# Attention and two expert layers on one core: row tiles 2 and 3 of the first batch spread over 16 half steps, and the next batch's bounds at other heads

## The chip, the core and the metric

The kernel runs on one core of a Trainium2 chip, as one program. Times are microseconds of device time. TensorE multiplies matrices into PSUM, VectorE and ScalarE work on SBUF and PSUM, GpSimd works on SBUF, and SyncE (SP) holds one queue that issues the DMAs of this kernel. Each engine runs its own instructions strictly in order and waits on semaphores for the others.

The number to predict is the median of several executions of the changed kernel. For the kernel before, three executions gave 873.21, 873.78 and 876.23, with the median 873.78.

## The reference

Causal attention with a decay per position comes first (4 batches, 8 heads, 576 positions, 64 wide), and its output, 2304 tokens of 512, goes through two layers with two weights each:

```python
def _attn_ref(q, k, v, f):
    scores = scale * np.matmul(q, k.transpose(0, 1, 3, 2))
    cum = np.cumsum(np.log(np.clip(f, 0.0001, 1.0)), axis=-1)
    scores = np.where(causal, -1000000000.0, scores + cum[:, :, :, None] - cum[:, :, None, :])
    attn = np.exp(scores - np.max(scores, axis=-1, keepdims=True))
    return np.matmul(attn / (np.sum(attn, axis=-1, keepdims=True) + 1e-09), v)

def _moe_ref(x, w_in, w_out):                 # 512 -> 2048 -> 512
    h = x @ w_in
    sp = np.where(h > 20.0, h, np.log1p(np.exp(np.minimum(h, 20.0))))
    return (h * np.tanh(sp)) @ w_out

def _moe2_ref(x, w_in, w_out, g_ln):          # 512 -> 1024 -> 512
    h = x @ w_in
    solu = h * softmax(h)
    return (layernorm(solu) * g_ln) @ w_out
```

The first layer is called MoE in the names. Its weights arrive as 64-bit floats.

## The kernel before

**Splits.** All products run in fp16 with every operand split into a high and a low half (`x = hi + lo`); three of the four products are kept. So each tile passes a cast (high half) and a subtract (low half), and each scale that keeps the halves in range is a power of two worked out from the data: for the weights from a bound per group, for q, k and v from squares summed over each batch (`stats`, `across`, `scales`).

**Attention.** The rows of a batch are cut into tiles 0 to 4 of up to 128 rows. `seq` lists *slots*: of tile 0 four heads make one slot, of tile 1 two, of tiles 2 to 4 one, so 2 + 4 + 8 + 8 + 8 = 30 slots for each batch. I write (3,7) for head 7 of row tile 3. A slot has the scores on TensorE (`step_s`, L409 to L412), the row max on VectorE and the exp on ScalarE (`step_r`, L451 and L453; for tile 4 L464 to L468), the high half by a cast (`step_h`, L491, in the first batch on ScalarE) and the low half on GpSimd (L492). Two heads share one tile `ph` and one transpose by DMA (L497, result `pT`). Three slots later (LAG = 3) come the products with v (`step_pv`, P.V, L523 to L525). After a row tile's last head `fin` scales the sum (x, L538), casts (L541) and subtracts (L542), and a DMA transposes the result into `xT` of the MoE block that holds these rows (L550). The next row tiles are prepared by `ahead`, head by head: raw q, k, v are loaded into a pool of three buffers, statistics are taken, scales are set, and the tiles are split.

**MoE blocks.** A block holds 256 tokens, so nine blocks in all; block 1 needs row tiles 2 and 3 of batch 0. A block has 16 units n. `up(n)` is 12 matmuls (L753), a pair of units shares the activation, called mish (`mish_a`, `mish_b`, `mish_c`: ScalarE L765 to L773, VectorE `ta` L770 and `th` L774, the cast to `gt` L779, its low half on GpSimd L780), and `down(n)` is six matmuls (L797). Block 0 runs while the weights are still prepared, in four groups of the two weights: load, conversion to fp32 by three bit operations on VectorE (L135, L137, L139), a Gram matmul (L158), the bound (L173 to L178), and the halves `win` and `wout` (L196 to L204), some on VectorE and ScalarE and some on ScalarE and GpSimd. The strings W1P and W2P set who does which half.

**The order of the work.** The code is one long loop over half steps. In each half step `hn` it issues an up or a down, up to four weight steps, and as many attention slots as `att_slots(hn)` asks for, a running total. That function spreads the cost of all slots evenly over EB = 190 half steps (`goal`), asks for enough slots in the last six half steps of a block that the next one can start (`lo`, from `need`), and never runs too far ahead (`hi`). The instructions are then put in order on each engine by a scheduler with a model of time, so that the order on the engines follows the code only roughly.

## Time and profile before

| | us |
|---|---|
| median of three executions | 873.78 |
| profiled execution | 870.92 |
| its span | 869.1 |
| TensorE busy in it | 747.8 (86%) |
| VectorE busy | 612.1 (70%) |
| ScalarE busy | 548.2 (63%) |
| GpSimd busy | 440.8 (51%) |

The span is the time from the first to the last instruction of the profiled execution. A busy share over the whole span is a mean over stages with different limits, so the stages are read apart: the first batch's preparation (to about 75 us), the weights of the MoE layer with block 0 beside them (to about 160), attention and blocks 1 to 8 (to about 550), the second layer's weights and the last blocks (to about 625), and the second layer.

### The profile page before, as it was taken

The numbers are of one execution on the slowest core, as the hardware profiler recorded it, in microseconds if no ns is written. First come the engines' busy times: TensorE is split into PE (matmuls) and PEld (weight loads), VectorE is DVE, ScalarE is ACT, GpSimd is POOL, SyncE is SP. The second block draws the span as 40 slices with busy tenths as digits, with TensorE's granted clock in tenths as the row PEclk, the third lists the DMA queues.
The fourth block names the chain that finished last, engine by engine and source line by source line (L and its number), as shares of the span: only waits on it lengthen the run. The fifth ranks groups of instructions, "written<-read, shape, count | busy, mean of one in ns | idle before, by whom it ended". The sixth has DMA issues, their size and how long they took to land.

```text
span 869.1 us, 16449 instructions
## 1 busy us (share of the span) xinstructions
PE 747.8 (86%) x6174; PEld 479.0 (55%) x6174; DVE 612.1 (70%) x1158; ACT 548.2 (63%) x1202; POOL 440.8 (51%) x341
## 2 busy tenths in 40 slices
PE   0546777778999989999888999986999999999997
PEld 0445445556667666677656766653555554444443
DVE  6799997577957978857896754689666454666451
ACT  5644638858778877698866767686965544333331
POOL 2269576635777678764777653227733132012110
PEclk9999887879999999999899999999999999999999
DMA  9999434668889799997897633761022523354543
GB/s 242 227 242 236 161 142 85 129 104 146 160 161 187 142 169 164 179 183 129 169 173 116 129 69 67 184 214 63 25 37 61 97 49 74 85 109 99 108 89 82
DMA packets 328571, 114.88 MB, mean 132 GB/s; under 512 B 317676, under 2 KB 317676, under 8 KB 328492
## 3 DMA queue, kind: packets, MB, share of 16 engines
q1 hardware_dynamic: 328492, 113.84, 62.5%
q8 instruction: 48, 0.79, 0.4%
q14 instruction: 31, 0.25, 0.1%
HBM read 46.59 MB, written 9.55 MB: 65 GB/s over the span
## 4 chain that ended last, share of the span: by engine, by line
PE 31%; DVE 25%; DMA 16%; ACT 9%; issue 9%; POOL 8%; SPq 1%; DVEq 0%; POOLq 0%; ACTq 0%
PE h L994 10%; PE o L1034 10%; DMA pT<-ph 6%; PE x L797 5%; PE h L753 4%; POOL ph L492 3%; DMA kt<-kn 2%; DVE ta L770 2%; DVE th L774 2%; DVE ph L489 2%; ACT p L453 2%; DMA w2i_r<-in_moe_w_in_dram 2%; DVE wout L137 1%; POOL gt L780 1%; DMA qa<-qn 1%
## 5 line engine op out<-in xcount | busy, mean ns | idle before, releaser
L753 PE MATMUL h<-xT,win 128*128 128x256 f16 x1728 | 225.0, 281 | 10.5 <-POOL win L204 4.0
L797 PE MATMUL x<-wout,gt 128*128 128x512 f16 x864 | 218.8, 387 | 16.2 <-ACT gt L779 5.9
L753 PEld LDWEIGHTS <-win 128*128 128x128 f16 x1728 | 170.9, 101 | 53.2 <-POOL win L204 4.2
L492 POOL TENSOR_TENSOR ph<-p,ph 128x512 f16<-128x512 f32 (+4 forms) x120 | 157.1, 1315 | 68.4 <-ACT ph L491 31.0
L780 POOL TENSOR_TENSOR gt<-th,gt 128x512 f16<-128x512 f32 x72 | 93.4, 1298 | 113.1 <-ACT gt L779 113.1
L797 PEld LDWEIGHTS <-gt 128*128 128x128 f16 x864 | 80.9, 100 | 94.7 <-issue 12.2
L1022 POOL TENSOR_TENSOR z<-sl,z 128x1024 f16<-128x1024 f32 x18 | 38.7, 2151 | 138.1 <-DVE s2c L1001 111.3
L523 PE MATMUL pv<-vt,pT 128*128 128x64 f16 (+3 forms) x480 | 72.7, 205 | 33.1 <-DMA pT<-ph 29.8
L994 PE MATMUL h<-w,x2T 128*128 128x512 f16 x432 | 98.4, 380 | 2.9 <-POOL w L204 1.6
L1034 PE MATMUL o<-wo,zT 128*128 128x512 f16 x432 | 96.5, 379 | 0.5 <-DMA zT<-z 0.5
L774 DVE SCALAR_TENSOR_TENSOR th<-ta,th 128x512 f32<-128x512 f32 x72 | 66.9, 930 | 27.6 <-ACT ta L773 27.3
L409 PE MATMUL sp<-kt,qa 128*128 128x128 f16 (+3 forms) x480 | 72.9, 225 | 13.4 <-ACT p L453 6.2
L453 ACT ACTIVATE p<-sp,nm 64x64 f32<-64x64 f32 (+7 forms) x128 | 61.2, 482 | 34.0 <-DVE nm L451 20.2
L523 PEld LDWEIGHTS <-pT 128*128 128x128 f16 (+3 forms) x480 | 46.5, 103 | 54.4 <-DMA pT<-ph 38.3
L410 PE MATMUL sp<-kt,qb 67*128 67x128 f16 (+3 forms) x480 | 73.7, 226 | 2.9 <-DVE qb L398 2.4
L770 DVE TENSOR_SCALAR ta<-ta 128x512 f32<-128x512 f32 x72 | 58.7, 815 | 21.8 <-ACT ta L765 21.5
L524 PE MATMUL pv<-vt,pT 128*128 128x64 f16 (+3 forms) x480 | 71.7, 200 | 0.6 <-DVE vt L197 0.6
L994 PEld LDWEIGHTS <-x2T 128*128 128x128 f16 x432 | 42.4, 98 | 53.9 <-issue 4.0
L525 PE MATMUL pv<-vt,pT 128*128 128x64 f16 (+3 forms) x480 | 71.8, 201 | 0.0
L1034 PEld LDWEIGHTS <-zT 128*128 128x128 f16 x432 | 42.2, 98 | 51.4 <-DMA zT<-z 0.9
L779 ACT CAST gt<-th 128x512 f16<-128x512 f32 x72 | 44.3, 615 | 41.3 <-DVE th L774 38.5
L771 ACT ACTIVATE ta<-ta 128x512 f32<-128x512 f32 x72 | 45.4, 631 | 35.0 <-DVE ta L770 34.8
(235 smaller groups left out, 1460.0 us busy)
## 6 DMA issues: line engine op xcount, KB each, us to landing
wi_r<-in_moe_w_in_dram SPq DMA_DIRECT2D x8, 1024.0 KB, 5.0
wo_r<-in_moe_w_out_dram SPq DMA_DIRECT2D x8, 1024.0 KB
rawk<-in_k_dram SPq DMA_DIRECT2D x25, 256.0 KB, 4.1
rawv<-in_v_dram SPq DMA_DIRECT2D x25, 256.0 KB, 4.1
x2d<-x2h SPq DMA_DIRECT2D x18, 256.0 KB, 2.4
out_dram<-ro SPq DMA_DIRECT2D x18, 256.0 KB, 2.0
w2i_r<-in_moe_w_in_dram SPq DMA_DIRECT2D x4, 1024.0 KB, 9.7
w2o_r<-in_moe_w_out_dram SPq DMA_DIRECT2D x4, 1024.0 KB, 5.0
```

The lines of the kernel that those rows point to most:

```text
L409: nc.tensor.matmul(o, qa[:, h, r0:r1_], kc[:, h, a0:a1], start=True, stop=False)
L410: nc.tensor.matmul(o, qb_[:67, h, r0:r1_], kc[:67, H + h, a0:a1], start=False, stop=(c != i))
L453: nc.scalar.activation(pv[:m, g * (i + 1) * P + off:g * (i + 1) * P + end], s3[:, g, off:end], AF.Exp, bias=nm[:m, g:g + 1], accum_out=rs[ ...
L492: nc.gpsimd.tensor_tensor(p4[:, :, 1], pv3, p4[:, :, 0], op=ALU.subtract)
L523: nc.tensor.matmul(o, pT[a0:a1, k, :m], vh, start=(c == 0), stop=False)
L753: nc.tensor.matmul(ph, win[:, (fi // 4) * NC1 + c, col:col + P], x[:, lx * NC1 + c, :], start=(m == 0), stop=(m == 3 * NC1 - 1))
L770: nc.vector.tensor_scalar(ta, ta, E20, 1.0, op0=ALU.min, op1=ALU.add)
L774: nc.vector.scalar_tensor_tensor(th, ta, 2.5, th, op0=ALU.subtract, op1=ALU.mult)
L780: nc.gpsimd.tensor_tensor(gt[:, 1], th, gt[:, 0], op=ALU.subtract)
L797: nc.tensor.matmul(o, gt[:, lg, n % 2, t * P:(t + 1) * P], wout[:, fi, lw * 512:(lw + 1) * 512], start=(first and m == 0), stop=(last and ...
L994: nc.tensor.matmul(h[:, half * 512:(half + 1) * 512], x[:, lx * NC1 + c, :], self.w2[:, half * NC1 + c, lw * 512:(lw + 1) * 512], start=(n ...
L1034: nc.tensor.matmul(o, zT[:, lz * NF2 + c, :], self.wo[:, c, lw * 512:(lw + 1) * 512], start=(n == 0), stop=(n == 3 * NF2 - 1))
```

## The change

Two things change. `att_slots` gets another lower limit in block 0: in each of its first 16 half steps (A0) one more slot is asked for, so that the 16 slots of row tiles 2 and 3 of batch 0 are issued at an even rate. Before, the even pace by cost set them. And `ahead` issues the loads, statistics and scales of the next batch's k and v at other heads: it counts from row tile 2 instead of tile 3, with the loads at counts 6, 8, 14, 15, 16, the statistics at 8, 10, 15, 16, 17, and the scales at 18. Counted in the same way, before they stood at 8, 10, 12, 14, 16, at 10, 12, 14, 16, 18, and at 19. The load of the next batch's row tile 0 goes from head 4 to head 3 of row tile 4, and its split from head 5 to head 4. The strings that set who does which half of the weights are the same in both.

```diff
+A0 = 16
...
-        if b + 1 < B and i in (3, 4):
-            n = (i - 3) * H + h
-            if n in (0, 2, 4, 6, 8):
-                load_raw(b + 1, n // 2, "kv")
-            if n in (2, 4, 6, 8, 10):
-                stats(b + 1, n // 2 - 1, "kv")
-            if n == 11:
+        if b + 1 < B and i in (2, 3, 4):
+            n = (i - 2) * H + h
+            if n in (6, 8, 14, 15, 16):
+                load_raw(b + 1, (6, 8, 14, 15, 16).index(n), "kv")
+            if n in (8, 10, 15, 16, 17):
+                stats(b + 1, (8, 10, 15, 16, 17).index(n), "kv")
+            if n == 18:
                 scales(b + 1, "kv")
         if nb < B:
-            if h == (LD if ni else 12 - H) and nb > 0:
+            if h == (LD if ni else 3) and nb > 0:
                 load_raw(nb, ni, "qkv")
...
-            if h == (LD + 2 if ni else 5):
+            if h == (LD + 2 if ni else 4):
...
         lo = need[j + 1] + LAG if j + 1 < NBLK and r >= 2 * NF1 - ATE else 0
+        if j == 0:
+            lo = max(lo, n0 + LAG + min(need[1] - n0, (r + 1) * (need[1] - n0) // A0))
         hi = need[j + XB] - 1 if j + XB < NBLK else len(seq) + LAG
```

The change adds one line at the top and two near the end, so a line L451 of before is L452 in the changed kernel, and L865 is L868.

The scheduler turns this into another order on the engines. Three places matter here. The first is VectorE around the bound of the last weight group of w_in, the row L178 before and L179 now (`wi_b`; `wo_r7` is the last raw tile of w_out, `nm_0_3_1` the row max of batch 0's head (3,1), `x32_0_2` the output of row tile 2). Before:

```order
L137 SCALAR_TENSOR_TENSOR wout_94<-wo_r7_881,wout_94 128x1024
L97 TENSOR_SCALAR wi_b_157<-wi_b_157 128x1
L770 TENSOR_SCALAR ta_4_1438<-ta_4_1438 128x512
L451 TENSOR_REDUCE nm_0_2_7_1026<-sp2_148 128x1
L451 TENSOR_REDUCE nm_0_3_0_1095<-sp0_146 128x1
L139 SCALAR_TENSOR_TENSOR wout_94<-wo_r7_881,wout_94 128x1024
L177 RECIPROCAL wi_b_157<-wi_b_157 128x1
L589 COPY wpt_83<-wi_b_157 128x1
L398 COPY qb0_126<-qa_0_4_1342 64x8x64
L197 SCALAR_TENSOR_TENSOR wout_94<-wout_94,wo_b_158 128x2x512
L535 TENSOR_SCALAR rr_0_2_1186<-rsum_0_2_613 128x8
L178 TENSOR_SCALAR wi_b_157<-wi_b_157 128x1
```

And now:

```order
L96 TENSOR_SCALAR wi_b_157<-wi_b_157 128x1
L198 SCALAR_TENSOR_TENSOR wout_94<-wout_94,wo_b_158 128x2x512
L452 TENSOR_REDUCE nm_0_3_0_1063<-sp0_146 128x1
L452 TENSOR_REDUCE nm_0_3_1_1090<-sp1_147 128x1
L542 CAST xh_0_2_1145<-x32_0_2_1143 128x512
L140 SCALAR_TENSOR_TENSOR wout_94<-wo_r7_917,wout_94 128x1024
L98 TENSOR_SCALAR wi_b_157<-wi_b_157 128x1
L775 SCALAR_TENSOR_TENSOR th_5_1660<-ta_5_1659,th_5_1660 128x512
L178 RECIPROCAL wi_b_157<-wi_b_157 128x1
L590 COPY wpt_83<-wi_b_157 128x1
L174 TENSOR_REDUCE wo_b_158<-gram_150 128x1
L179 TENSOR_SCALAR wi_b_157<-wi_b_157 128x1
```

The bound is the sixth row behind the last bit operation on the weights (L139, now L140) in both. Ahead of that operation the max of (3,1) and the cast of row tile 2's output have come in, and between it and the bound the `th` of units 10 and 11. Just above the second piece stand the `th` of units 8 and 9, the `ta` of units 10 and 11 and `x32_0_2`, all of which stood behind the bound before. The max of (2,7) moved further up.

The second place is GpSimd around the halves of the same group (`win_93` the halves of w_in, `wout_94` of w_out, `gt_4` the activation of units 8 and 9). Before:

```order
L201 TENSOR_SCALAR win_93<-win_93 128x2x512
L204 TENSOR_TENSOR win_93<-win_93 128x2x512
L542 TENSOR_TENSOR xh_0_2_1191<-x32_0_2_1189,xh_0_2_1191 128x512
L201 TENSOR_SCALAR wout_94<-wout_94 128x2x512
L201 TENSOR_SCALAR win_93<-win_93 128x2x512
L780 TENSOR_TENSOR gt_4_1482<-th_4_1439,gt_4_1482 128x512
L204 TENSOR_TENSOR wout_94<-wout_94 128x2x512
L492 TENSOR_TENSOR ph_0_3_0_1101<-p32_1_129,ph_0_3_0_1101 128x4x128
L492 TENSOR_TENSOR ph_0_3_2_1204<-p32_0_128,ph_0_3_2_1204 128x4x128
L204 TENSOR_TENSOR win_93<-win_93 128x2x512
L780 TENSOR_TENSOR gt_5_1676<-th_5_1593,gt_5_1676 128x512
```

And now:

```order
L781 TENSOR_TENSOR gt_4_1636<-th_4_1608,gt_4_1636 128x512
L543 TENSOR_TENSOR xh_0_2_1145<-x32_0_2_1143,xh_0_2_1145 128x512
L493 TENSOR_TENSOR ph_0_3_0_1066<-p32_0_128,ph_0_3_0_1066 128x4x128
L493 TENSOR_TENSOR ph_0_3_0_1066<-p32_1_129,ph_0_3_0_1066 128x4x128
L781 TENSOR_TENSOR gt_5_1689<-th_5_1660,gt_5_1689 128x512
L202 TENSOR_SCALAR win_93<-win_93 128x2x512
L205 TENSOR_TENSOR win_93<-win_93 128x2x512
L202 TENSOR_SCALAR wout_94<-wout_94 128x2x512
L202 TENSOR_SCALAR win_93<-win_93 128x2x512
L205 TENSOR_TENSOR wout_94<-wout_94 128x2x512
L493 TENSOR_TENSOR ph_0_3_2_1158<-p32_0_128,ph_0_3_2_1158 128x4x128
L205 TENSOR_TENSOR win_93<-win_93 128x2x512
```

Three splits are made here, of two rows each (L201 and L204). Before, row tile 2's output, a `gt` and two low halves of attention stood among them. Now two `gt`, row tile 2's output and two low halves of attention stand ahead of the first of them, and one low half among them.

The third place is ScalarE ahead of the exp of (3,7), the last head that block 1 needs (`ta_6` and `ta_7` are the mish of units 12 to 15, `jkv` the statistics of raw values). Before, behind the first mish step of `ta_6`, its partner L766 and the exp of (3,5):

```order
L313 ACTIVATE jkv_1_4_1641,st_1_1162<-rawv_1_4_1531 128x512
L771 ACTIVATE ta_6_1726<-ta_6_1726 128x512
L765 ACTIVATE ta_7_1863<-h_0_14_1751,usc1_0_79 128x512
L766 ACTIVATE th_7_1864<-h_0_14_1751 128x512
L453 ACTIVATE p32_0_128,rsum_0_3_1094<-sp0_146,nm_0_3_6_1435 128x512
L491 CAST ph_0_3_4_1312<-p32_1_129 128x4x128
L772 ACTIVATE ta_6_1726<-ta_6_1726,c_k1_72 128x512
L771 ACTIVATE ta_7_1863<-ta_7_1863 128x512
L491 CAST ph_0_3_6_1443<-p32_0_128 128x4x128
L773 ACTIVATE ta_6_1726<-ta_6_1726 128x512
L772 ACTIVATE ta_7_1863<-ta_7_1863,c_k1_72 128x512
L453 ACTIVATE p32_1_129,rsum_0_3_1094<-sp1_147,nm_0_3_7_1479 128x512
```

And now, from the first mish step of `ta_6` on:

```order
L766 ACTIVATE ta_6_1732<-h_0_12_1676,usc1_0_79 128x512
L767 ACTIVATE th_6_1733<-h_0_12_1676 128x512
L492 CAST ph_0_3_4_1238<-p32_1_129 128x4x128
L454 ACTIVATE p32_0_128,rsum_0_3_1062<-sp0_146,nm_0_3_6_1333 128x512
L772 ACTIVATE ta_6_1732<-ta_6_1732 128x512
L766 ACTIVATE ta_7_1863<-h_0_14_1757,usc1_0_79 128x512
L767 ACTIVATE th_7_1864<-h_0_14_1757 128x512
L492 CAST ph_0_3_6_1341<-p32_0_128 128x4x128
L773 ACTIVATE ta_6_1732<-ta_6_1732,c_k1_72 128x512
L454 ACTIVATE p32_1_129,rsum_0_3_1062<-sp1_147,nm_0_3_7_1374 128x512
```

The exp of (3,7) stood as the fourteenth instruction behind the first mish step of `ta_6`, and now stands as the ninth. The exp of (3,5), the statistics and three mish steps went to other places.

## Rows read from the trace of the kernel before

**Rows 1.** First line of the page: span and instructions of the profiled execution
```profile
span 869.1 us, 16449 instructions
```

**Rows 2.** Table of stretches: stretch, length, busy time by engine, clock, DMA share, GB/s
```profile
75.00:135.00 60.00, 43.91 (x332) 29.66 (x329) 59.02 (x76) 31.10 (x49) 40.42 (x20) 0.89 0.48 156
135.00:191.00 56.00, 40.02 (x408) 28.51 (x407) 34.71 (x83) 42.30 (x98) 34.93 (x26) 0.78 0.62 112
191.00:550.00 359.00, 331.70 (x3541) 237.38 (x3542) 269.00 (x490) 274.54 (x669) 235.62 (x209) 0.98 0.79 144
550.00:869.00 319.00, 303.13 (x1618) 158.46 (x1615) 186.96 (x401) 157.82 (x287) 94.98 (x56) 0.99 0.38 92
```

**Rows 3.** TensorE in time: start, us, line, output and inputs, count, [idle before]
```profile
155.27 1.49 PE L753 MATMUL h<-xT,win 128*128 128x256 f16 x12 [1.49 <-POOL win L204]
...
176.27 1.89 PE L797 MATMUL x<-wout,gt 128*128 128x512 f16 x8
...
178.00 0.19 PE L523 MATMUL pv<-vt,pT 128*128 128x64 f16 x1
...
191.42 0.82 PE L753 MATMUL h<-xT,win 128*128 128x256 f16 x3 [1.83 <-DMA xT<-xh]
```

**Rows 4.** GpSimd in time, same columns, 137 to 185 us
```profile
137.75 1.05 POOL L201 TENSOR_SCALAR win<-win 128x1024 f16<-128x1024 f32 x1 [0.41 <-ACT win L199]
...
143.10 1.16 POOL L542 TENSOR_TENSOR xh<-x,xh 128x512 f16<-128x512 f32 x1 [2.09 <-DVE xh L541]
...
146.25 1.59 POOL L780 TENSOR_TENSOR gt<-th,gt 128x512 f16<-128x512 f32 x1
...
149.88 2.27 POOL L492 TENSOR_TENSOR ph<-p,ph 128x512 f16<-128x512 f32 x2
...
152.11 3.10 POOL L204 TENSOR_TENSOR win<-win 128x1024 f16<-128x1024 f32 x1
...
168.84 2.51 POOL L492 TENSOR_TENSOR ph<-p,ph 128x512 f16<-128x512 f32 x2
...
184.68 1.72 POOL L542 TENSOR_TENSOR xh<-x,xh 128x512 f16<-128x512 f32 x1 [4.22 <-DVE xh L541]
```

**Rows 5.** VectorE in time, 116 to 181 us
```profile
116.14 0.54 DVE L451 TENSOR_REDUCE nm<-sp 128x1 f32<-128x384 f32 x1
...
116.61 2.61 DVE L139 SCALAR_TENSOR_TENSOR win<-wi_r,win 128x1024 int32<-128x1024 int32 x1
...
132.60 1.21 DVE L139 SCALAR_TENSOR_TENSOR wout<-wo_r,wout 128x1024 int32<-128x1024 int32 x1
...
136.06 0.14 DVE L178 TENSOR_SCALAR wi_b<-wi_b 128x1 f32<-128x1 f32 x1
...
140.22 1.33 DVE L774 SCALAR_TENSOR_TENSOR th<-ta,th 128x512 f32<-128x512 f32 x1
...
151.14 2.10 DVE L197 SCALAR_TENSOR_TENSOR wout<-wout,wo_b 128x1024 f16<-128x1024 f32 x1 [4.31 <-ACT wout L196]
...
157.73 1.11 DVE L770 TENSOR_SCALAR ta<-ta 128x512 f32<-128x512 f32 x1 [3.30 <-ACT ta L765]
...
158.89 0.69 DVE L451 TENSOR_REDUCE nm<-sp 128x1 f32<-128x512 f32 x1
...
180.40 0.68 DVE L538 TENSOR_TENSOR x<-pv,rr 128x512 f32<-128x512 f32 x1
```

**Rows 6.** ScalarE in time, 149 to 204 us
```profile
149.20 0.63 ACT L313 ACTIVATE jkv<-rawv 128x512 f32<-128x512 f32 x1 [1.72 <-DMA rawv<-in_v_dram]
...
157.01 0.69 ACT L765 ACTIVATE ta<-h,usc 128x512 f32<-128x512 f32 x1 [0.97 <-PE h L753]
...
164.88 0.70 ACT L453 ACTIVATE p<-sp,nm 128x512 f32<-128x512 f32 x1
...
203.24 0.31 ACT L453 ACTIVATE p<-sp,nm 64x64 f32<-64x64 f32 x1 [0.35 <-DVE nm L451]
```

**Rows 7.** Waits of TensorE: waiter, awaited, us in all, times, longest
```profile
PE pv L523 <- DMA pT<-ph: 29.8, 24, 3.5
```

## The prediction

> **What bounds the kernel now.** I read the table of stretches first, then the starts of TensorE's matmul groups, then the instructions of each engine between 100 and 205 us, and the order of both kernels at the same places. The span is 869.1 us [rows 1]. TensorE is busy 331.70 of the 359 us from 191 to 550, and 303.13 of the last 319 [rows 2]: there it is the bound, and an edit can win little. Before 191 it is not. Between 75 and 135 VectorE is, with 59.02 busy of 60: it converts the MoE weights, and attention and block 0 wait behind that. From 135 to 191 TensorE is busy only 40.02 of 56 us and VectorE 34.71: no engine is full, and what the reader is to see is a chain. The first ups that need the last weight group start at 155.27, after 1.49 of waiting for a half that GpSimd splits; block 1's first up starts at 191.42, after waiting for the transposed attention output xT [rows 3]. In the 36 us between, block 0 ends and slots of row tile 4 run. The chain that ends at 191.42, followed back: GpSimd's low half of the output at 184.68 [rows 4], the scaled output x on VectorE at 180.40 [rows 5], P.V of heads 6 and 7 of row tile 3 at 178.00 [rows 3], GpSimd's low half of head (3,7) at 168.84 [rows 4], its exp at 164.88 [rows 6], its row max at 158.89 [rows 5]. Row tile 3 is that late because head 6 of row tile 2 got its max only at 116.14, behind weight steps, and because several maxima of tile 3 stand behind a wout step at 151.14 that had waited 4.31 for ScalarE [rows 5]; ScalarE had stood still until 149.20 for a raw value load of the next batch [rows 6].
>
> The profiled execution took 870.92 us, its span and 1.8 around it; the median of the runs is 873.78, 2.86 higher. I sum against 870.92 and add 2.86 at the end. What starts block 1 earlier is handed on nearly whole: from the 24th up on TensorE's order is the same in both, and it is nearly full from there.
>
> **Row tiles 2 and 3 in 16 half steps.** The change issues one slot in each of block 0's first 16 half steps; no computation is added or removed. On VectorE the max of (2,6) moves ahead of a weight conversion, and (3,5) stands ahead of the wout step of 151.14 instead of behind it. The wout step itself I leave at 151: it still waits for ScalarE behind the statistics of a raw tile, whose load stands on SP behind a transpose of row tile 3. So the start of block 1 moves link by link:
> - The max of (3,7) follows the wout step (151.14 + 2.10) and (3,6), 0.69 each, so it is at about 154.6; before, it stood behind a ta that waited 3.30 for ups [rows 5]. From there ScalarE's order decides. Between its first mish step of units 12 and 13 at 157.01 and the exp of (3,7) at 164.88 [rows 6] lay 13 instructions, 7.87 / 13 = 0.61 each; now there are 8. The five that went (the exp of (3,5), a statistic, three mish steps) are 3.0. The mish step itself comes 0.7 earlier (154.5 against 155.2, under the last weight group below). I take 3.7 (1 to 4.4).
> - From that exp to the end of the low half were 5.2 us (168.84 and half of 2.51, [rows 4]). A gt of 1.1 that stood ahead on GpSimd now stands behind, and fewer exps of row tile 4 lie between on ScalarE. I take 1.5 (0 to 2).
> - From there to P.V were 7.9 us: the transpose, and downs in front of P.V on TensorE. The group now stands behind down 14, before behind down 16. Eight matmuls of downs took 1.89 at 176.27 [rows 3]; a down has six, so two are 2.8. The transpose may come later than these, so I take 1.9 (0 to 2.8).
> - From x at 180.40 to the low half at 184.68 [rows 4, 5] are 4.3 us. A row max (0.69) and a scaling of raw q, about as long, no longer stand between x and its cast: 1.4 (0 to 1.5).
> Sum: 3.7 + 1.5 + 1.9 + 1.4 = 8.5. Block 1 would start at about 182.9.
>
> The other half of the pace is batch 1's attention, whose first exp ran at 203.24 [rows 6]. It gains less: on ScalarE the scaling of the next q tile, which needs a load issued late, now stands before the exps of head (4,3), where it stood behind those of (4,5). I take 7 (0 to 9). TensorE alternates between both, so the end gains between 7 and 8.5; I take 7.7.
>
> **The last weight group.** Its bound on VectorE was ready at 136.06 [rows 5]. Ahead of it now stand two th steps (1.33 each), a ta (1.11), an x (0.68), its cast and one max (taken at 0.69 each); a max of heads (2,7), taken at 0.6, went away. 2 x 1.33 + 1.11 + 0.68 + 0.69 + 0.69 - 0.6 = 5.2 later. GpSimd took from 137.75 to 155.2 (152.11 + 3.10) over the halves of this group, with 2.09 idle and 1.16 + 1.59 + 2.27 = 5.0 of attention and gt work among them [rows 4]. All but one low half of that now stands ahead of them: 17.45 - 2.09 - 5.0 + 1.14 = 11.5 remain, and 137.75 + 5.2 + 11.5 = 154.5. I cost the edit at nothing beyond the 0.7 above; its cover is GpSimd's idle time and the rows that went ahead. Without that cover it costs the 5.2.
>
> **The bounds of the next batch.** As many loads, statistics and scales as before. Of the five pairs of loads the first three go earlier, the last two come in consecutive heads, and the scales come one head earlier, as do the load and the split of each next batch's first tile. On SP the early raw loads of batch 1 now stand ahead of weight loads and of the transpose of row tile 2's output; SP had room there. Two later boundaries follow (three with the first, which is in the sum above). TensorE's waits for attention transposes were 29.8 in 24, 1.24 each and 3.5 at the longest [rows 7]; one longest stop more or less at each boundary is -7.0 to +7.0, one mean stop -2.5 to +2.5. The rows are nearer to the mean, and loads bunch as much as scales gain: I take 0.
>
> **A rule weighed.** In the weight stretch an or of VectorE (two tiles in, one out) takes 2.61 at 116.61, when GpSimd works on a 128x1024 subtract, and 1.21 at 132.60, when it doesn't [rows 5]. Three attention subtracts, of heads (2,6), (2,7) and (3,0), move further into that stretch, where VectorE is full; I price one by 2.27 / 2 = 1.14 [rows 4].
> The Trainium skill, page "SBUF — State Buffer", section "Who interferes with whom", says that a VectorE instruction with two SBUF inputs and a GpSimd instruction that reads SBUF contend for one shared port pair, and that whoever comes first holds it for the whole instruction. By that rule each moved subtract is paid by VectorE in full, which the 2.61 against 1.21 bears out. It is the third rival.
>
> **Rivals.**
> - A slower one: the last weight group decides. If the gt steps and low halves that now stand ahead of it on GpSimd have to wait for ScalarE, the cover is gone: the last split ends 5.2 later, and all that follows it in order moves with it, up 12, the first mish step of its pair, and the exp of (3,7), which stands behind that on ScalarE. 873.78 + 5.2 = 879.0. For it: GpSimd's rows run in order, and 2.09 of its idle time there was a wait of this kind. Against: the 154.5 above. It decides once the last split ends after about 160.
> - No change: xT is earlier, but batch 1's attention is not, because ScalarE waits for raw q ahead of (4,3) and TensorE then stops at the first P.V of batch 1: 873.8 less 0 to 2.6. For it: the scaling of q moves ahead of three heads' exps. Against: the scales of batch 1, and with them its first q tile, come earlier as well.
> - VectorE pays for GpSimd: the bounds of groups 2 and 3 come three subtracts later, 3 x 1.14 = 3.4, and 7.7 - 3.4 = 4.3 of the gain remain: 869.5. For it: 2.61 against 1.21. Against: those subtracts met the same kind of step before, only later, so the sum of such meetings may not grow.
> - A bigger gain: the whole chain at its better ends (4.4 + 2 + 2.8 + 1.5 = 10.7) and a mean stop less at both boundaries, 2.5: 873.8 - 13.2 = 860.6.
>
> **How the numbers follow.** Forecast 870.92 - 7.7 + 2.86 = 866.1. Chances: forecast (a gain of 5 to 10) 0.43; half the gain by contention 0.14; a bigger gain 0.08; no change 0.16; slower 0.19. Two medians of this kernel can be told apart beyond 0.3%, 2.6 us. Faster: 0.43 + 0.14 + 0.08 = 0.65; same 0.16; slower 0.19. The range goes from a little beyond the bigger gain, since its two parts may meet the attention's gain of 9 as well, 858, to 877, most of the way to the slower rival; beyond these I leave 0.04 and 0.12. The likeliest case alone has 863 to 869.
>
> **What would show it.** Right: the max of (3,7) before 156 and its exp before 162, P.V of (3,6) by 171.5, block 1's first up between 181 and 185, batch 1's first exp by 198, and everything after 225 shifted by 6 to 9. For the weight step: the last split of win done by 156. Wrong: that split past 160 with block 0's last ups behind it (the slower rival); block 1 at 183, but a stop of over 4 us on TensorE before 225 (no change); ors and conversions of weight group 2 at 2.6 and more where they had 1.2 (contention). The forecast falls as a whole if TensorE's order after the 24th up isn't what carries the gain on: then block 1 starts early and a later stage stands where it stood.

## The result

The changed kernel took 861.34 us (858.52 to 864.30, four runs) against 874.56 before (873.21 to 876.23, four runs): a ratio of 0.9848, with an interval from 0.9809 to 0.9887. A second series gave 860.93 and 0.9856 (0.9824 to 0.9889). It is 13 us faster. Forecast were 7.7 less, 866.1, with 858 to 877 as the range, and 863 to 869 for the likeliest case: the range holds the time, the likeliest case does not. The profiled execution took 862.0, 8.9 less than the one of before, which at 870.92 had been quicker than most of its kind.

The head of the page of the changed kernel (span; then busy time, share and instructions of each engine), and its table of stretches, with the columns of [rows 2]:

```profile
span 860.2 us, 16457 instructions
...
PE 748.2 (87%) x6174; PEld 477.6 (56%) x6174; DVE 606.7 (71%) x1158; ACT 549.1 (64%) x1202; POOL 442.2 (51%) x341
```

```profile
75.00:135.00 60.00, 43.49 (x348) 30.28 (x346) 59.72 (x75) 33.79 (x54) 42.69 (x22) 0.91 0.59 176
135.00:191.00 56.00, 43.77 (x407) 30.03 (x405) 41.82 (x90) 42.30 (x97) 37.18 (x25) 0.79 0.61 115
191.00:550.00 359.00, 338.81 (x3588) 239.41 (x3588) 261.83 (x490) 276.72 (x670) 235.12 (x209) 0.98 0.79 148
550.00:860.00 310.00, 292.65 (x1568) 152.95 (x1565) 182.88 (x397) 152.98 (x277) 92.80 (x54) 0.99 0.37 87
```

TensorE's busy time is the same as before (748.2 against 747.8); what is gained is time in which it stood still, 9.3 us less than before in these two profiles. From 135 to 191 it is busy 43.77 against 40.02, from 191 to 550 338.81 against 331.70 [rows 2].

The links of the chain, engine by engine. TensorE, with the columns of [rows 3]: P.V of heads 6 and 7 of row tile 3, a stop, and block 1's first up.

```profile
172.53 0.19 PE L524 MATMUL pv<-vt,pT 128*128 128x64 f16 x1
...
181.71 0.22 PE L410 MATMUL sp<-kt,qa 128*64 128x128 f16 x1 [3.16 <-ACT p L469]
...
184.38 1.04 PE L754 MATMUL h<-xT,win 128*128 128x256 f16 x4
```

GpSimd, as [rows 4]: the last split of w_in, the low half of head (3,7), and the low half of row tile 3's output.

```profile
153.00 2.12 POOL L205 TENSOR_TENSOR win<-win 128x1024 f16<-128x1024 f32 x1
...
165.94 1.30 POOL L493 TENSOR_TENSOR ph<-p,ph 128x512 f16<-128x512 f32 x1 [1.90 <-ACT ph L492]
...
178.56 1.72 POOL L543 TENSOR_TENSOR xh<-x,xh 128x512 f16<-128x512 f32 x1 [1.80 <-DVE xh L542]
```

VectorE, as [rows 5]: the bound of the last group of w_in, the wout step, the max of (3,7), and the output of row tile 3.

```profile
141.59 0.14 DVE L179 TENSOR_SCALAR wi_b<-wi_b 128x1 f32<-128x1 f32 x1
...
153.14 3.06 DVE L198 SCALAR_TENSOR_TENSOR wout<-wout,wo_b 128x1024 f16<-128x1024 f32 x1 [1.86 <-ACT wout L197]
...
158.07 0.69 DVE L452 TENSOR_REDUCE nm<-sp 128x1 f32<-128x512 f32 x1 [1.26 <-ACT p L454]
...
175.30 0.69 DVE L539 TENSOR_TENSOR x<-pv,rr 128x512 f32<-128x512 f32 x1
```

ScalarE, as [rows 6]: the exp of (3,5), the first mish step of units 12 and 13, the exp of (3,7), the scalings of batch 1's second q tile and second k tile, and batch 1's first exp.

```profile
157.25 0.69 ACT L454 ACTIVATE p<-sp,nm 128x512 f32<-128x512 f32 x1 [2.75 <-POOL ph L493]
...
158.30 0.69 ACT L766 ACTIVATE ta<-h,usc 128x512 f32<-128x512 f32 x1 [0.26 <-PE h L754]
...
163.24 0.70 ACT L454 ACTIVATE p<-sp,nm 128x512 f32<-128x512 f32 x1
...
179.91 0.72 ACT L197 ACTIVATE qn<-rawq,scu 128x512 f16<-128x512 f32 x1 [3.33 <-DMA rawq<-in_q_dram]
...
183.28 0.71 ACT L197 ACTIVATE kn<-rawk,scu 128x512 f16<-128x512 f32 x1
...
199.40 0.31 ACT L454 ACTIVATE p<-sp,nm 64x64 f32<-64x64 f32 x1
```

| | before | predicted | after |
|---|---|---|---|
| bound of the last group of w_in | 136.06 | 141.3 | 141.59 |
| end of its last split | 155.2 | 154.5 | 155.12 |
| max of (3,7) | 158.89 | 154.6 | 158.07 |
| exp of (3,7) | 164.88 | 161.2 | 163.24 |
| end of its low half | 170.1 | 164.9 | 167.24 |
| P.V of (3,6) and (3,7) | 178.00 | 170.9 | 172.53 |
| output x of row tile 3 | 180.40 | 173.3 | 175.30 |
| its low half | 184.68 | 176.2 | 178.56 |
| block 1's first up | 191.42 | 182.9 | 184.38 |
| batch 1's first exp | 203.24 | 196.2 | 199.40 |

The chain is the one that was predicted, and its end within 1.5 us. Only its last link has changed: the first up no longer waits for xT, as no idle time stands before it at 184.38; it follows scores of row tile 4 that TensorE had reached after 3.16 of waiting for an exp. But the chain does not explain 13 us, and that it is handed on had to be tested.

### The profile page after: what moved, and what is told of

The parts are those of the page before. It is cut to its first block, busy times and chain, and to the rows that moved or that the text cites. A ratio compares the mean times of both kernels' runs of the same rounds, so it can differ in the third digit from the quotient of the medians.

```text
span 860.2 us, 16457 instructions
## 1 busy us (share of the span) xinstructions
PE 748.2 (87%) x6174; PEld 477.6 (56%) x6174; DVE 606.7 (71%) x1158; ACT 549.1 (64%) x1202; POOL 442.2 (51%) x341
## 4 chain that ended last, share of the span: by engine, by line
PE 40%; DVE 23%; DMA 13%; ACT 9%; issue 8%; POOL 7%; SPq 1%; POOLq 0%; DVEq 0%; ACTq 0%
PE h L997 10%; PE o L1037 10%; PE x L798 9%; PE h L754 7%; DMA pT<-ph 4%; POOL ph L493 4%; DVE th L775 3%; DVE ta L771 2%; DMA w2i_r<-in_moe_w_in_dram 1%; DVE wout L140 1%; PE pv L524 1%; DVE ph L490 1%; DVE wout L138 1%; POOL gt L781 1%; DMA rawk<-in_k_dram 1%
## 5 line engine op out<-in xcount | busy, mean ns | idle before, releaser
L798 PE MATMUL x<-wout,gt 128*128 128x512 f16 x864 | 222.1, 392 | 21.8 <-ACT gt L780 10.1
L493 POOL TENSOR_TENSOR ph<-p,ph 128x512 f16<-128x512 f32 (+4 forms) x120 | 159.6, 1334 | 80.3 <-ACT ph L492 32.8
L524 PE MATMUL pv<-vt,pT 128*128 128x64 f16 (+3 forms) x480 | 71.0, 203 | 15.4 <-DMA pT<-ph 10.7
L775 DVE SCALAR_TENSOR_TENSOR th<-ta,th 128x512 f32<-128x512 f32 x72 | 69.4, 965 | 21.1 <-ACT ta L774 20.9
L525 PE MATMUL pv<-vt,pT 128*128 128x64 f16 (+3 forms) x480 | 70.1, 198 | 1.0 <-DVE vt L198 1.0
L526 PE MATMUL pv<-vt,pT 128*128 128x64 f16 (+3 forms) x480 | 70.3, 198 | 0.0
L771 DVE TENSOR_SCALAR ta<-ta 128x512 f32<-128x512 f32 x72 | 53.7, 745 | 16.6 <-ACT ta L766 16.2
```

The source lines that it names most:

```text
L493: nc.gpsimd.tensor_tensor(p4[:, :, 1], pv3, p4[:, :, 0], op=ALU.subtract)
L524: nc.tensor.matmul(o, pT[a0:a1, k, :m], vh, start=(c == 0), stop=False)
L526: nc.tensor.matmul(o, pT[a0:a1, k + 1, :m], vh, start=False, stop=(c == i))
L771: nc.vector.tensor_scalar(ta, ta, E20, 1.0, op0=ALU.min, op1=ALU.add)
L775: nc.vector.scalar_tensor_tensor(th, ta, 2.5, th, op0=ALU.subtract, op1=ALU.mult)
L798: nc.tensor.matmul(o, gt[:, lg, n % 2, t * P:(t + 1) * P], wout[:, fi, lw * 512:(lw + 1) * 512], start=(first and m == 0), stop=(last and ...
```

## How the traces are compared

TensorE does the same matmuls in all kernels here, so its progress can be compared. As the reference serves a second profile of the kernel before, of 873.52 us, near the median (run e10 below). I sum the columns of all matmuls that the reference has started by a time, and ask how much earlier the other kernel had started the same sum. That is its *lead* at this time, in us; it counts attention and MoE alike. Each run is named by its parts: P the pace of block 0, F the new heads for the bounds of batch 1, L those for batches 2 and 3. The move of the load and the split of row tile 0 (from heads 4 and 5 to 3 and 4) is in all variants but the pace alone, and has no letter: without it the order is the same on every engine, instruction for instruction. Last come two columns of the rows themselves: the start of block 1's first up, and the first exp of batch 1's row tile 4.

```
lead in us at ...          210   230   260   340   400   430   530    up     exp
before, first profile      0.4   1.5   3.4   2.8   3.6   3.8   2.8   191.4  277.9
before, e10                  0     0     0     0     0     0     0   192.3  281.4
PFL (the change)           9.9   6.1   7.6   3.6   4.5  10.3  11.6   184.4  272.8
PFL, e1                   10.6   8.8   9.0   4.4   5.1  10.8  12.7   183.7  271.9
P, e2                     14.0   8.9   7.6   2.7   4.2   3.6   3.6   180.9  275.0
P, e11                    14.2   9.1   7.8   3.0   5.1   4.6   6.6   181.3  274.8
L, e3                      0.6  -0.3   3.1  -2.4  -3.2   1.9   3.5   192.6  277.9
PF, e4                     9.7   8.9   9.0   7.5   9.8   8.4  10.3   185.1  271.5
PF + batch 3 of L, e8     11.7   9.6  12.1   9.7  11.4  14.0  13.0   183.6  269.9
PL, e6                    15.1   9.1   8.2   3.6   2.8   5.5   2.9   180.3  275.1
FL, e7                    12.8   3.0   2.5  -3.0  -1.9   0.7   0.5   182.9  279.2
FL, e12                   12.1   2.3   1.6  -3.8  -2.7  -1.1   0.2   184.0  280.0
PFL, start delayed, e9     1.4   3.0   6.3   0.2   0.0   5.6   6.6   194.4  276.3
PFL, x delayed, e5         1.2   1.5   3.4  -4.2  -5.5  -1.9  -0.8   195.9  278.4
```

## The experiments

Theory A is the prediction's own: what block 1 gains at its start is handed on to the end. Its first rival, B, came from the first profile of the change, whose gain over the first profile of before shrank to about 1 us between 340 and 410 and came back at the boundary of batch 2 to batch 3.

**e1: the change again.** No edit.

> The changed kernel once more, for a second profile of it. Both theories expect 859 to 864 (0.982 to 0.988 of before). They differ in the trace. Theory A (handed on): what block 1 gains at its start, 7 us, is carried to the end; the fading of the lead to about 1 us between 340 and 410 us, which the first profile shows, is chance of that one execution, and in this profile TensorE's lead over the kernel before stays at 5 us or more from 230 to 410. Theory B (the last boundary): the lead fades here too, to 3 us or less between 340 and 410, and comes back to 8 or more after the boundary of batch 2 to batch 3 at about 415.

Measured: 860.93, 0.9856 (0.9824 to 0.9889). The lead falls to 4.4 at 340 (1.6 over the first profile of before) and comes back to 10.8 at 430 here too. So the fading is not chance; this claim of theory A fell.

**e2: the pace alone.**

```diff
# against the changed kernel: ahead() as in the kernel before
-        if b + 1 < B and i in (2, 3, 4):
+        if b + 1 < B and i in (3, 4):
...
```

> Only the 16 even half steps of block 0; loads, statistics and scales of the next batch at the heads of before, at all three boundaries. Theory A (handed on): block 1 starts 6 to 8 us earlier than before and the end gains 6 to 9: 0.990 to 0.993 of before, 865 to 868. Theory B (the last boundary): block 1 starts just as early, the lead fades before 410, and since the bounds are the old ones nothing comes back: 0.997 to 1.000, 871 to 875.

Measured: 867.91, 0.9929 (0.9906 to 0.9952), 6 us faster than before, as A had it and not as B had it. Block 1 starts 3 us earlier still than in the change.

**e3: the later bounds alone.**

```diff
# against the kernel before: the new heads only for batches 2 and 3
+        if b > 0 and b + 1 < B and i in (2, 3, 4):
...
-        if b + 1 < B and i in (3, 4):
+        if b == 0 and b + 1 < B and i in (3, 4):
```

> Block 0's pace and the bounds of batch 1 as in the kernel before; only the bounds of batches 2 and 3 at the new heads. On every engine the order is that of before up to about 240 us. Theory A (handed on): the start of block 1 is as before, so nothing is gained: 0.997 to 1.003, 871 to 877. Theory B (the last boundary): the stop of before at 412 to 417 (0.79 and 2.29) goes, and the end gains 4 to 8: 0.991 to 0.996, 866 to 870.

Measured: 873.71, 1.0011 (0.9985 to 1.0037). No gain, as A had it; B falls. The trace shows why B had seemed right: against e10 the new heads cost 6 us of lead between 260 and 400 and give it back by 530.

**e4: the pace with the bounds of batch 1.**

```diff
# against the changed kernel
-        if b + 1 < B and i in (2, 3, 4):
+        if b == 0 and b + 1 < B and i in (2, 3, 4):
...
+        if b > 0 and b + 1 < B and i in (3, 4):   # the heads of before
```

> The changed kernel with the bounds of batches 2 and 3 put back to the heads of before; the order is that of the changed kernel up to about 230 us on every engine. Theory A (handed on): the end keeps the start's gain: 860 to 866, within 3 us of the changed kernel. Theory B (the last boundary): the lead fades by 410 and does not come back: 868 to 873, 6 us or more above the changed kernel.

Measured: 864.93, 0.9894 (0.9863 to 0.9924). A's range holds, though not its "within 3 us" (it is 4 above the change); B's does not. The lead stays between 7.5 and 10.3 from 210 to the end. From here to the change are 4 us, from the pace alone 3; the intervals of neighbours overlap, so neither step is clear by itself.

**e5: the output of row tile 3 delayed on GpSimd.** The edit repeats one subtract, with the same result.

```diff
         nc.gpsimd.tensor_tensor(xh[:m, 1], x32[:m], xh[:m, 0], op=ALU.subtract)
+        for _ in range(4 if (b, i) == (0, 3) else 0):
+            nc.gpsimd.tensor_tensor(xh[:m, 1], x32[:m], xh[:m, 0], op=ALU.subtract)
```

> The changed kernel, in which GpSimd makes the low half of row tile 3's output five times instead of once: four times 1.15 to 1.7 more, 4.6 to 6.8 us, in the middle of the chain to block 1's first up, with nothing else added. Theory A (handed on): the first up starts 5 to 7 us later, at about 190, and the end is 3 to 7 us above the changed kernel: 864 to 868. Theory C (slack): the start of block 1 has slack, batch 1's attention sets the pace there, and the end is within 2 us of the changed kernel: 859 to 863.

Measured: 877.0, 1.0029 (1.0002 to 1.0056): 16 us above the change, more than either theory allows. GpSimd's rows (start, us), and SP's transpose of the output, show that the edit did more than it should (L545 are the extra subtracts, L493 low halves of row tile 4):

```profile
178.00 1.15 POOL L543 TENSOR_TENSOR xh<-x,xh 128x512 f16<-128x512 f32 x1 [1.81 <-DVE xh L542]
...
182.93 1.74 POOL L493 TENSOR_TENSOR ph<-p,ph 64x640 f16<-64x640 f32 x1 [0.97 <-ACT ph L492]
...
185.75 1.83 POOL L493 TENSOR_TENSOR ph<-p,ph 64x640 f16<-64x640 f32 x1
...
187.55 1.59 POOL L545 TENSOR_TENSOR xh<-x,xh 128x512 f16<-128x512 f32 x1
...
191.43 1.28 SPq L553 DMA_TRANSPOSE xT<-xh  x1
```

The extra subtracts stand among low halves of row tile 4, so attention waits as well; the transpose comes at 191.43, where e1 had it at 179.59. The run hits both streams and tells nothing of the start alone. e9 tries it in another way.

**e6: the pace with the later bounds only.**

```diff
# against the changed kernel: the new heads only for batches 2 and 3
-        if b + 1 < B and i in (2, 3, 4):
+        if b > 0 and b + 1 < B and i in (2, 3, 4):
...
```

> The changed kernel with only batch 1's bounds put back to the heads of before; batches 2 and 3 keep the new ones. Theory A (handed on), in the form the first four runs left it: without the early bounds the first q tile of batch 1 is scaled at about 182 instead of 173, TensorE waits for k and q of batch 1 near 199 and 217 as in the run with the pace alone, and the result is like that run: 0.991 to 0.995, 866 to 870. Theory D (three independent parts): the pace is worth 6, batch 1's bounds 3 and the later bounds 4, each alone, so this kernel gains 10: 0.987 to 0.990, 863 to 865.

Measured: 871.37, 0.9986 (0.9962 to 1.0010): no gain that can be told from none. Theory D falls; A named the mechanism (below), but it expected 4 us at least. On the pace alone the later bounds even cost 3.5 us (867.91 in e2, 871.37 here), and the two intervals do not overlap. Block 1's first up is the earliest of all runs, 180.3. Ten us lie between this kernel and the change, and all that differs is the bounds of batch 1.

What these do is seen in the second profile of the pace alone (e11). In the order of ScalarE the scalings of batch 1's first two q tiles and of its second k tile come late, and TensorE waits (start, us, line):

```profile
182.14 0.72 ACT L197 ACTIVATE qn<-rawq,scu 64x512 f16<-64x512 f32 x1
...
192.99 0.72 ACT L197 ACTIVATE qn<-rawq,scu 128x512 f16<-128x512 f32 x1
...
195.79 0.72 ACT L197 ACTIVATE kn<-rawk,scu 128x512 f16<-128x512 f32 x1
...
201.53 0.32 PE L410 MATMUL sp<-kt,qa 128*128 128x128 f16 x2 [2.74 <-DMA kt<-kn]
...
218.76 0.22 PE L411 MATMUL sp<-kt,qb 67*128 67x128 f16 x1 [1.69 <-DVE kt L375]
```

TensorE then stands 2.74 for k of row tile 1 and 1.69 for row tile 2. With the bounds early the two q tiles are scaled at 173.77 and 179.91 in the change, 8 and 13 us sooner, that k tile at 183.28 instead of 195.79, and these two stops are gone. In e6 they are there as in e11, with one more of 2.05 for k at 202.86 (TensorE):

```profile
200.33 0.32 PE L410 MATMUL sp<-kt,qa 128*128 128x128 f16 x2 [2.49 <-DMA kt<-kn]
...
218.81 0.22 PE L411 MATMUL sp<-kt,qb 67*128 67x128 f16 x1 [1.69 <-DVE kt L375]
```

**e7: all new bounds without the pace.**

```diff
# against the changed kernel
-        if j == 0:
-            lo = max(lo, n0 + LAG + min(need[1] - n0, (r + 1) * (need[1] - n0) // A0))
```

> All bounds at the new heads, without the even pace of block 0. Theory A (handed on): row tile 3 of batch 0 is as late as before, block 1 cannot start earlier, and early bounds of batch 1 meet attention that is not there yet: 0.997 to 1.003, 871 to 877. Theory D (three independent parts): 3 for the first bounds and 0 to 4 for the later ones, 0.992 to 0.997, 867 to 871.

Measured: 874.49, 1.0013 (0.9993 to 1.0034). The time is A's, the reason is not. A had expected block 1 to start late; it starts at 182.87, earlier than in the change, TensorE is 12.8 ahead at 210, and nothing of that reaches the end. In the rows of TensorE, SP's queue and ScalarE (the second q tile of batch 1, and the exp of (4,5)):

```profile
182.87 0.50 PE L754 MATMUL h<-xT,win 128*128 128x256 f16 x3
...
176.37 1.23 SPq L551 DMA_TRANSPOSE xT<-xh  x1
179.84 1.20 SPq L374 DMA_TRANSPOSE kt<-kn  x1
181.07 1.27 SPq L396 DMA_TRANSPOSE qa<-qn  x1
182.39 0.58 SPq L300 DMA_DIRECT2D rawq<-in_q_dram  x1
...
185.87 0.72 ACT L197 ACTIVATE qn<-rawq,scu 128x512 f16<-128x512 f32 x1 [0.53 <-DMA rawq<-in_q_dram]
...
188.28 0.29 ACT L468 ACTIVATE p<-sp,nm 64x64 f32<-64x64 f32 x1
```

SP issues the output's transpose first and the load of the second q tile at 182.39; ScalarE scales it at 185.87, and the exp of (4,5), behind it in order, is at 188.28, not earlier than in the kernel before (187.47 and 188.17 in its two profiles). In the change the same load is issued ahead of the output's transpose, at 175.83 in e1 (SP):

```profile
174.59 1.19 SPq L396 DMA_TRANSPOSE qa<-qn  x1
175.83 0.57 SPq L300 DMA_DIRECT2D rawq<-in_q_dram  x1
```

So here the early start and an attention as late as before come together, and the time is that of the rival called no change. That the one makes the other worthless is argued, not shown: TensorE's stops in this profile are 1.72 at 199.41 and 1.03 at 207.66 for transposes of row tile 4, and 1.74 at 222.67 for batch 1's row tile 1, none of them the single stop of over 4 us that the rival had named.

**e8: pace, and the bounds of batches 1 and 3.**

```diff
# against the changed kernel: batch 2 at the heads of before
-        if b + 1 < B and i in (2, 3, 4):
+        if b != 1 and b + 1 < B and i in (2, 3, 4):
...
+        if b == 1 and b + 1 < B and i in (3, 4):   # the heads of before
```

> The pace, and the bounds of batches 1 and 3 at the new heads, those of batch 2 at the heads of before. Up to about 370 us the order is that of the run without the later bounds, whose lead stayed near 6 there, while the changed kernel's faded to about 1 between 280 and 410. Theory E (a price at one boundary, a gain at the next): batch 2's new bounds cost 3 to 5 us between 280 and 340 and batch 3's give 3 to 5 after 410, so this kernel beats the changed one: 856 to 859. Theory A (handed on, the rest is chance of the order): it lands between the two, 861 to 866.

Measured: 861.81 (861.78 to 862.90), 0.9871 (0.9844 to 0.9898). That is in A's range and no better than the change, so batch 2's new heads neither cost nor give at the end and theory E's gain is not there, though the lead does what E said up to 400 (11.4 against 4.5 and 5.1). What the change has lost by then it makes up by 430; the stops that the kernel before has at that place (TensorE in e10) are absent from it.

```profile
417.40 0.19 PE L409 MATMUL sp<-kt,qa 128*64 128x64 f16 x1 [1.01 <-ACT p L468]
...
420.32 0.23 PE L523 MATMUL pv<-vt,pT 64*128 64x64 f16 x1 [2.31 <-DMA pT<-ph]
```

**e9: the start of block 1 delayed by a detour of its input.**

```diff
         nc.gpsimd.tensor_tensor(xh[:m, 1], x32[:m], xh[:m, 0], op=ALU.subtract)
+        if (b, i) == (0, 3):
+            for z in range(1):
+                nc.scalar.dma_start(dz, xh)      # dz: a new tile in DRAM
+                nc.scalar.dma_start(xh, dz)
```

> The changed kernel, in which the output of row tile 3 goes to DRAM and back before its transpose (two DMAs of 256 KB on ScalarE's queue): block 1's first up comes 4 to 6 us later, at 188 to 191, near where the kernel before had it, and batch 1's attention, with its bounds early, waits for nothing new; in TensorE's order its first scores now stand ahead of that up. Theory A (handed on): the start's 7 us are most of the gain, so the end is 4 to 6 us above the changed kernel: 865 to 868. Theory F (attention paces): the start of block 1 has slack as long as row tiles 1 to 3 of batch 1 come as early as in the changed kernel (first exp of row tile 3 at 243 to 246), and the end is within 2 us of it: 859 to 863.

Measured: 866.86, 0.9930 (0.9911 to 0.9950), 6 us above the change. The start came later than meant, 10 us behind the change and 2 to 3 behind the kernel before:

```profile
191.54 0.26 PE L525 MATMUL pv<-vt,pT 128*64 128x64 f16 x1 [3.96 <-DMA pT<-ph]
...
194.42 1.89 PE L759 MATMUL h<-xT,win 128*128 128x256 f16 x8
```

Yet the kernel is 6 us faster than before. A's time holds, though for a delay of 10 and not 4 to 6; F's does not, and its condition was not met either: batch 1's row tile 3 began at 246.95. Nor was attention left alone, as was meant: on ScalarE the second q tile of batch 1 is scaled at 181.88, behind the exp of (4,3), and not at 179.91 ahead of it; TensorE waits 3.96 for a transpose of row tile 4; and batch 1's first exp comes at 201.80, 2 to 3 us behind the change (199.40, and 198.71 in e1) and about 2 ahead of the kernel before. So the run delays the start by 10 us and attention by 2 to 3, and does not separate the two.

**e10: the kernel before again.**

> The kernel before once more, for a second profile: the first one took 870.92, less than most of its runs (median 874). Both theories expect 870 to 877. If it takes 873 or more, its trace shows where a usual run loses the 3 us that the first profile did not: theory A expects them before 225 us, theory F in the attention of batches 1 to 3, between 225 and 540.

Measured: 873.52. It is behind the first profile by 2 to 3 us, all of which arise by 260 (the table's first line: 0.4 at 210, 3.4 at 260). Half of that is before 230 and half behind it, so it speaks for neither theory. Measured against this profile, the leads at 530 agree with the timed medians: 12.7 for e1 (13), 6.6 for e11 (6), 10.3 for e4 (9), 6.6 for e9 (6).

**e11: the pace alone again.**

> The pace alone once more, for a second profile: the first took 869.77, the slowest of its five runs. Expected 866 to 870. In both theories block 1's first up is at 180 to 182 and TensorE waits for k of batch 1 near 199 and 217; theory F expects the first exp of batch 1's row tile 3 at 247 to 251, no earlier than in the kernel before by more than 2.

Measured: 867.18. First up at 181.34, stops at 201.53 and 218.76 as shown above, first exp of row tile 3 at 250.55: as expected.

**e12: all new bounds without the pace, again.**

> All bounds at the new heads without the pace, once more, for a second profile: there block 1's first up came as early as with the pace, TensorE was 12 us ahead of the kernel before at 205, and 9 of that were gone at 220. Expected 872 to 877. Theory G (clock): the granted clock from 200 to 210 is 0.6 or less again, as in the first profile (0.50), and TensorE does not stand still for more than 4 us between 200 and 225. Theory F (attention paces): the clock there is above 0.8 in this execution, the 9 us go all the same, and TensorE stands waiting for transposes of batch 0's row tile 4 and of batch 1 instead.

Measured: 873.77. One execution of the kernel before, taken beside it, took 880.54, above all its others here (869.16 to 878.37); no ratio is made from these two. The stretches of e7 (columns as in [rows 2]; the granted clock is the third number from the right):

```profile
190.00:200.00 10.00, 8.09 (x111) 6.96 (x108) 6.96 (x19) 10.00 (x22) 3.82 (x3) 1.00 1.02 177
200.00:210.00 10.00, 8.20 (x74) 5.20 (x74) 6.11 (x10) 6.71 (x28) 7.94 (x8) 0.50 0.78 160
210.00:220.00 10.00, 10.00 (x94) 6.29 (x94) 9.24 (x12) 8.68 (x20) 5.14 (x5) 0.81 0.39 81
220.00:230.00 10.00, 8.26 (x75) 5.56 (x73) 7.66 (x11) 4.56 (x11) 6.98 (x6) 0.83 1.01 153
```

And those of e12, with two of its stops on TensorE:

```profile
190.00:200.00 10.00, 9.75 (x137) 8.45 (x134) 6.87 (x19) 10.00 (x23) 3.69 (x3) 1.00 0.92 191
200.00:210.00 10.00, 6.54 (x71) 4.01 (x71) 6.33 (x11) 7.82 (x29) 8.84 (x9) 0.79 0.83 154
210.00:220.00 10.00, 9.88 (x89) 6.08 (x87) 9.25 (x12) 7.68 (x19) 4.10 (x4) 0.87 0.35 72
220.00:230.00 10.00, 7.36 (x58) 5.01 (x59) 7.66 (x11) 4.45 (x11) 6.41 (x6) 0.66 0.95 152
```

```profile
202.59 0.19 PE L410 MATMUL sp<-kt,qa 128*128 128x64 f16 x1 [1.31 <-ACT p L454]
...
204.50 1.04 PE L798 MATMUL x<-wout,gt 128*128 128x512 f16 x4 [1.29 <-ACT gt L780]
```

The granted clock from 200 to 210 was 0.50, the level of 1.2 GHz all through, in e7, and 0.79 in e12; yet the lead fell alike, from 12.8 to 3.0 and from 12.1 to 2.3 by 230. In this stretch more standing went with the higher clock (8.20 busy of 10 in e7, 6.54 in e12); from 220 to 230 e12 had both the lower clock and the more standing. Neither theory's numbers were met: no 0.6 again, and not above 0.8. G also expected at most 4 us of standing, and e12 has 6.2 from 200 to 230. The clock is not the cause by itself; stops and clock share the loss in different parts.

## Why the prediction was right, and where not

**The chain to block 1.** Right in its links and within the bounds given for each: 7.0 gained of 8.5. The four terms of the sum, 3.7, 1.5, 1.9 and 1.4, measured 1.6, 1.2, 2.6 and 1.0; 0.9 more came at the last link, the first up itself, and 0.4 was lost between P.V and x. The first term was off most. The eight instructions from the mish step to the exp of (3,7) took 4.94, as forecast, but the mish step came at 158.30, 1.3 later than before and not 0.7 earlier. It waited last, by 0.26, for the up of unit 12. The ups behind the last split start at 155.18, as before (155.27), but their 28 matmuls took 4.61 us where they had taken 3.23: TensorE had stood still for 1.80 before 153.90 and 0.59 before 155.18, and the granted clock from 155 to 158 was 0.50, the level of 1.2 GHz, where it had been 1.00.

```profile
155.18 4.61 PE L754 MATMUL h<-xT,win 128*128 128x256 f16 x28 [0.59 <-POOL win L205]
...
155.00:158.00 3.00, 2.82 (x14) 2.01 (x15) 1.81 (x2) 0.75 (x2) 3.00 (x3) 0.50 0.00 0
```

Quicker ups alone would have won 0.3 at most by these rows, as ScalarE was held until 157.9 by the exp of (3,5), which had waited 2.75 for a low half on GpSimd. The max of (3,7) waited 1.26 for the same exp and came at 158.07. The 154.6 of the forecast is where that max ends; its start by the same sum is 153.9, since 151.14 + 2.10 already ends the wout step and only one max, of 0.69, lies between. The wout step itself came at 153.14 and took 3.06. The bound of the last weight group came within 0.4 of the forecast and its split within 0.6; the slower rival's point, 160, was never near.

**Handed on nearly whole.** This step failed as it was put. The start of block 1 alone carries nothing: e7 and e12 start as early as the change and end with the kernel before; e9 starts behind the kernel before and is 6 us faster. Its premise was wrong too: TensorE's order is not the same from the 24th up on. Ahead of the 58th up, at 352.06 before and 364.36 now, stand 1511 matmuls of attention and 288 of downs in the kernel before, 1601 and 324 in the change. The prediction had said that it falls as a whole if this order isn't what carries the gain on; its time came out within the range all the same, with half of the gain from the bounds. What it said beside it, that TensorE alternates between block 1 and batch 1's attention, fits the runs better if the gain is not the mean of both but needs both. With block 1 early and attention late it is 0 (e7), 1 to 2 (e6) or 6 (the pace alone), with attention partly early and block 1 late 6 (e9), with both 9 (e4) to 13. This is a reading and not shown: the pace alone and e6 have the same first up and the same last column, and end 3.5 us apart, and no run moves one of the two alone. The last column of the table goes roughly with the times: from 269.9 to 272.8 for the kernels at 861 to 865, from 274.8 to 276.3 for those at 867 to 871, from 277.9 for those that gain nothing. It is a sign of how far attention has come, not shown to be the cause.

**The bounds at 0.** This is the term that was mis-sized. Of the first boundary I had only said that it was in the sum; by themselves the earlier bounds were costed at nothing, since as many instructions run. All bounds together gain 6 to 7 on top of the pace (867.9 to 861) and nothing without it (e7). On top of the pace and the later bounds those of batch 1 are worth 10 us (871.4 to 861), on top of the pace alone 3. The wait to look for stood in the trace of before, in the order of ScalarE: scaling k and q of the next batch stood behind exps of row tile 4, and the pace alone moves it further back, from 179.02 to 182.14. Before:

```profile
179.02 0.72 ACT L196 ACTIVATE qn<-rawq,scu 64x512 f16<-64x512 f32 x1
```

The later bounds are worth 3 to 4 behind the others, nothing alone, and 3.5 less than nothing on the pace alone; for the gain behind the others the intervals do not exclude none.

**Where the number came from.** The 7.7 stood for the pace with batch 1's bounds in it; these two together measured 9 (e4), the pace alone 6. The later bounds, priced at 0, gave about 4 more. That the range held the sum is in part luck: it reached down to 858 for a bigger gain, 860.6, to which I had given 0.08. The time landed there, but not by its way, which was a chain at its better ends (10.7 earlier, it was 7.0) and a mean stop less at both later boundaries.

**The rivals.** No change: its wait was there in the change too, 3.33 for raw q ahead of the scaling at 179.91 and then TensorE's 3.16 at 181.71, but not its sign, a stop of over 4 us; in e7 its time came, by several smaller stops and the clock. Contention: VectorE's ors of the weights with two tiles in (L137 and L139, now L138 and L140) took 32.6 us between 75 and 142 before (6.2 + 6.2 + 10.3 + 9.9) and 33.4 after (7.8 + 7.4 + 9.3 + 8.9). That is 0.8, not 3.4: those on w_in rose from 12.4 to 15.2, those on w_out fell from 20.2 to 18.2, and the bound of the third group came at 107.98, 3.6 earlier than before (111.59) and not later. The sign was there all the same, as single ones went from 1.2 to 3.1: the or of w_in at 112.37 before is at 116.36 now, beside a GpSimd subtract at 115.99. The Trainium skill (page "SBUF — State Buffer", section "Who interferes with whom") says that a VectorE instruction with two inputs in SBUF contends with a GpSimd instruction that reads SBUF; these single ones agree. That the moved subtracts met other steps than before, and not more of them, is how I read the sums. The slower one had no sign: the last split ended at 155.12 and not past 160.

**Of the signs named** the first up between 181 and 185 and the split by 156 came true. The max, the exp, P.V and the first exp of batch 1 came 1 to 2 us later than the limits given, and the shift behind 225 was not steady: against the first profile of before it was 2 to 3 at 300 and about 1 at 400.

What stays open: why the change loses 3 to 4 us of lead between 260 and 400, where e4 and e8 do not, and has it back by 430. The new heads of batch 2 go with the loss among these (e1, e3, e9 have it; e4 and e8 do not), but the pace alone, without them, loses as much (7.6 to 2.7 by 340 in e2, 7.8 to 3.0 in e11) and does not get it back. Which wait it is was not isolated. Open too is what takes e7's lead of 12.8 between 210 and 230.

## What to carry to other kernels

Where two streams share an engine, an earlier start of one is worth what the other lets it be: read the gate of each, and test them apart, before summing a gain along one chain. A part of a change that gains nothing alone, as the bounds do here without the pace, can be worth half of it together with another, so undo the parts one at a time from the whole as well as adding them one at a time. And take more than one profile of each kernel before placing a difference of 3 us.

## What was not expected of the hardware

Four more subtracts on GpSimd, 1.1 to 1.6 us each in e5, moved a transpose by 12 us (179.59 to 191.43): two low halves of attention (1.74 and 1.83) and a wait of 0.97 stand between them in GpSimd's order, and behind the last of them, which ended at 189.14, SP first issued the transposes of batch 1's k and q (188.16 and 190.03). And TensorE's granted clock differed between two executions of the same kernel in the same stretch (0.50 and 0.79 from 200 to 210) while the work done by 230 differed by 0.7 us.
